# Repacking the value and output projections of a memory-augmented segment recurrence into windows of 64 columns, and moving its mask to VectorE

## The chip, the cores and the metric

One core of a Trainium2 chip. The metric is the device time of one execution in microseconds, told as the median of the runs. A run is called slow only when it is over 1.5% above the fastest of its kernel.

## The reference, cut to what matters

Two layers A, each followed by a dense layer B. Layer A walks through 64 segments of 32 rows; each segment sees 8 rows of memory that the segment before it wrote.

(Shortened: names and shapes are simplified.)

```python
mem = mem0
for s in range(n_seg):                       # 64 segments of 32 rows
    h = concat([mem, x[s]])                  # 8 + 32 rows, 512 wide
    q, k, v = h @ Wq, h @ Wk, h @ Wv         # 32 heads of 128
    p = softmax(mask(q @ k.T * 128 ** -0.5)) # memory rows see all, row i sees keys up to i
    o = (p @ v) @ Wo
    mem = o[:8]                              # the next segment waits for this
    outs.append(o[8:])
x = x + A(layernorm(x)); x = x + B(layernorm(x)); and both once more
```

The memory is a chain: nothing of segment s + 1 that touches the memory can start before the output projection of segment s is done.

## The kernel before

Both layers run together. In step k (there are 69) layer 0 works on segment k and layer 1 on segment k - 5. The two segments share one operand HT of 80 columns: `[x0: 32 | mem0: 8 | mem1: 8 | x1: 32]`. Every operation is handed to a small list scheduler in the kernel, which assumes durations and fixes the order on each engine when the kernel is built; the chip runs each engine's list in order. The scheduler has a constant for TensorE that favours work which uses the array in the same split as the work before it (WHOLE, COL64: two column halves side by side, COL32: four quarters, ROW64: two row halves). Cut to the lines that the change touches; "..." marks what is left out.

```python
WHOLE, COL64, COL32, ROW64 = range(4)
TURN = 0.11      # what the scheduler thinks a change of split costs, us
STAY = 2.0       # how strongly it prefers not to change
...
# values of x, made ahead of the memory: 64 columns, 32 products in column halves (COL64)
nc.tensor.matmul(vx[64*b:64*b+64, :], lhsT=XS[:, c4, :], rhs=Wv_sb[:, c4, n*512:(n+1)*512], ..., tile_position=(0, 64*b))
...
# values of the two memories: 32 columns, four quarters (COL32)
nc.tensor.matmul(vm[32*q:32*q+32, :], lhsT=HT[:, c4, SEG:SEG+32], rhs=Wv_sb[:, c4, n*512:(n+1)*512], ..., tile_position=(0, 32*q))
# both reach the value tiles Vs[a] by DMA, 12 transfers per step
...
# scores: the mask is a matmul that starts the accumulation
nc.tensor.matmul(sp[64*g2:64*g2+64, ...], lhsT=ident[:, 64*g2:64*g2+64], rhs=maskb[...], start=True, stop=False, ...)
nc.tensor.matmul(v[64*g2:64*g2+L, a, b, ii, :], lhsT=QT[...], rhs=KT[...], start=False, ...)
# VectorE: maximum, subtract; ScalarE: exp; VectorE: sum, reciprocal; GpSimd: multiply
# turn of P: 128 columns, bf16 in PSUM; VectorE copies it to PT
nc.tensor.transpose(tp[...][:, z*128:(z+1)*128], P[:, a, ii, :, :]..., ident[:])
...
# next memory: 32 columns, COL32; copied out in two halves, picked and turned by a small product, then into HT
nc.tensor.matmul(wo[32*q:32*q+32, :], lhsT=OT[:, h, SEG:SEG+32], rhs=Wo_sb[:, h, :], ..., tile_position=(0, 32*q))
# projection of x: 32 columns per layer, COL32, awaited by nobody in this step
nc.tensor.matmul(wx[32*q:32*q+32, :], lhsT=OT[:, h, XO[a]:XO[a]+SEG], rhs=Wo_sb[:, h, :], ..., tile_position=(0, 32*q))
plan.op(DVE, t_dve(512), add, r=[wx, x], w=[("x", g, c)])     # four adds into x per step
```

Of the kernel before, what the change touches and what calls it, by code (L numbers as in the profile page):

```python
# [26 lines left out]
STAY = 2.0  # L27
# [143 lines left out]
def kernel(  # L171
# [34 lines left out]
    XO = (0, L + M)  # L206
    MO = (SEG, L)
    XR = (0, M)
    MR = (SEG, 0)
# [53 lines left out]
    maskb = sb("maskb", [128, 2, L])  # L263
    nc.gpsimd.memset(maskb[:], 0.0)
    for g2 in range(2):
        blk = maskb[64 * g2:64 * g2 + 64, 0, 0:SEG]
        nc.gpsimd.affine_select(out=blk, in_=blk, compare_op=ALU.is_ge, fill=NEG,
                                base=0, pattern=[[-1, SEG]], channel_multiplier=1)
        blk = maskb[64 * g2:64 * g2 + 64, 1, :]
        nc.gpsimd.affine_select(out=blk, in_=blk, compare_op=ALU.is_ge, fill=NEG,  # L270
                                base=0, pattern=[[-1, L]], channel_multiplier=1)
        nc.gpsimd.affine_select(out=blk, in_=blk, compare_op=ALU.is_ge, fill=0.0,
                                base=-M, pattern=[[0, L]], channel_multiplier=1)

    sel_f = sb("sel_f", [128, 2 * M], F32)
    nc.gpsimd.memset(sel_f[:], 0.0)
    for g in range(4):
        blk = sel_f[32 * g:32 * g + 32, :]
        nc.gpsimd.affine_select(out=blk, in_=blk, compare_op=ALU.not_equal, fill=1.0,
                                base=0, pattern=[[-1, 2 * M]], channel_multiplier=1)  # L280
    sel = sb("sel", [128, 2 * M])
    nc.vector.tensor_copy(out=sel[:], in_=sel_f[:])
# [4 lines left out]
    XSs = [sb(f"XS{i}", [128, NC4, 2 * SEG]) for i in range(2)]  # L287
    QT = sb("QT", [128, H, 2 * L])
    KT = sb("KT", [128, H, 2 * L])
    Vs = [sb(f"Vs{a}", [128, 4, 512]) for a in range(2)]  # L290
    PT = sb("PT", [128, 4, 2, 4, L])
    Pt = [sb(f"P{p}", [128, 2, 2, 2, 64]) for p in range(4)]
    vst = sb("vst", [128, 4, 512])
    vms = sb("vms", [128, 2, 512])
    OT = sb("OT", [128, H, 2 * L])
    wm = sb("wm", [128, Dm])
    for t in (*HTs, *XSs):
        nc.vector.memset(t[:], 0.0)
    for t in (*Pt, OT):
        nc.gpsimd.memset(t[:], 0.0)  # L300

    p_es = ring("es", 2, [128, 2, 2, 2, L], F32)
# [6 lines left out]
    b_qk, b_misc, b_st, b_fill = banks("qk", 2), banks("misc", 3), banks("st", 1), banks("fill", 2)  # L309
# [147 lines left out]
    def prep_x(k):  # L457

        act, seg = segs(k)
        i = k % 2  # L460
        HT, XS = HTs[i], XSs[i]
        for a in act:
            g, c = divmod(seg[a], GS)
            xnT = xnT_tiles[(a, g)]
            for key, dst in ((("XS", i, a), XS[:, :, SEG * a:SEG * (a + 1)]),
                             (("HTx", i, a), HT[:, :, XO[a]:XO[a] + SEG])):
                def cp(dst=dst, xnT=xnT, c=c):
                    nc.gpsimd.tensor_copy(out=dst, in_=xnT[:, :, SEG * c:SEG * (c + 1)])

                plan.op(POOL, 0.25, cp, r=[xnT], w=[key])  # L470
        for p in range(4):
            vx = b_fill.buf()

            def mm(vx=vx, p=p):
                for c4 in range(NC4):
                    for b in range(2):
                        n = 2 * p + b
                        nc.tensor.matmul(vx[64 * b:64 * b + 64, :], lhsT=XS[:, c4, :],  # L478
                                         rhs=Wv_sb[:, c4, n * 512:(n + 1) * 512],
                                         start=(c4 == 0), stop=(c4 == NC4 - 1), tile_position=(0, 64 * b))  # L480

            plan.op(PE, 0.216 * NC4, mm, r=[("XS", i, 0), ("XS", i, 1), ("W", "v", p)], w=[vx, ("vst", p)], tile=COL64)
            eng = ACT if p != 3 else DVE

            def ev(vx=vx, p=p, eng=eng):
                copy_on(eng, vst[:, p, :], vx[:, :])

            plan.op(eng, t_copy(eng, 512), ev, r=[vx], w=[("vst", p)])

    def place_x_values(k):  # L490
        act, _ = segs(k)
        for a in act:
            for b in range(2):
                def dma(a=a, b=b):
                    nc.sync.dma_start(out=Vs[a][64 * b + XR[a]:64 * b + XR[a] + SEG, :, :],
                                      in_=vst[64 * b + 32 * a:64 * b + 32 * a + SEG, :, :])

                plan.op(SP, 0.6, dma, r=[("vst", p) for p in range(4)], w=[("Vx", a, b)])

    def mem_values(k):  # L500

        act, _ = segs(k)
        i = k % 2
        HT = HTs[i]
        for pp in range(2):
            vm = b_st.buf()

            def mm(vm=vm, pp=pp):
                for c4 in range(NC4):
                    for q in range(4):  # L510
                        n = 2 * (2 * (q // 2) + pp) + q % 2
                        nc.tensor.matmul(vm[32 * q:32 * q + 32, :], lhsT=HT[:, c4, SEG:SEG + 32],  # L512
                                         rhs=Wv_sb[:, c4, n * 512:(n + 1) * 512],
                                         start=(c4 == 0), stop=(c4 == NC4 - 1), tile_position=(0, 32 * q))

            plan.op(PE, 0.216 * NC4, mm, r=[("HTm", i), ("HTx", i, 1), *[("W", "v", pc) for pc in range(4)]], w=[vm],
                    tile=COL32)
            eng = ACT if pp == 0 else DVE

            def ev(vm=vm, pp=pp, eng=eng):  # L520
                copy_on(eng, vms[:, pp, :], vm[:, :])

            plan.op(eng, t_copy(eng, 512), ev, r=[vm], w=[("vms", pp)])
        for a in act:
            for q in range(4):
                def dma(a=a, q=q):
                    b, p0 = q % 2, 2 * (q // 2)
                    nc.sync.dma_start(out=Vs[a][64 * b + MR[a]:64 * b + MR[a] + M, p0:p0 + 2, :],  # L528
                                      in_=vms[32 * q + M * a:32 * q + M * (a + 1), :, :])

                plan.op(SP, 0.63, dma, r=[("vms", 0), ("vms", 1)], w=[("Vm", a, q)])

    def queries_keys(k, hg, a_lo, a_hi):
# [4 lines left out]
        for nm, W_sb, dstT in (("q", Wq_sb, QT), ("k", Wk_sb, KT)):  # L538
            qp = b_qk.buf()

            def mm(qp=qp, W_sb=W_sb):
                for hi in range(4):
# [6 lines left out]
                    r=[("HTm", i), *[("HTx", i, a) for a in range(a_lo, a_hi)], ("W", nm, hg // 2)], w=[qp])  # L549
            eng = DVE if nm == "k" and hg % 4 != 1 else ACT  # L550

            def ev(qp=qp, dstT=dstT, eng=eng):
                copy_on(eng, dstT[:, 4 * hg:4 * hg + 4, c0:c1],
                        qp[:, 0:8 * L].rearrange("p (h n) -> p h n", h=4)[:, :, 0:n])

            plan.op(eng, t_copy(eng, 4 * n), ev, r=[qp], w=[(nm + "T", hg)])

    def scores(k, p, a_lo, a_hi):
# [3 lines left out]
        sp, mx, es, sm, tp = b_misc.buf(), p_mx.buf(), p_es.buf(), p_sm.buf(), b_misc.buf()  # L562
        P = Pt[p]

        def spv():
            return sp[:, 0:8 * L].rearrange("p (a b i k) -> p a b i k", a=2, b=2, i=2)

        def mm():
            for g2 in range(2):
                nc.tensor.matmul(sp[64 * g2:64 * g2 + 64, a_lo * 4 * L:a_hi * 4 * L],  # L570
                                 lhsT=ident[:, 64 * g2:64 * g2 + 64],
                                 rhs=maskb[:, a_lo:a_hi, :].unsqueeze(2).to_broadcast([128, na, 4, L]),
                                 start=True, stop=False, tile_position=(0, 64 * g2))
            v = spv()
            for a in range(a_lo, a_hi):
                for b in range(2):
                    for ii in range(2):
                        for g2 in range(2):
                            h = 8 * p + 4 * b + 2 * ii + g2
                            last = a == a_hi - 1 and b == 1 and ii == 1  # L580
                            nc.tensor.matmul(v[64 * g2:64 * g2 + L, a, b, ii, :], lhsT=QT[:, h, a * L:(a + 1) * L],  # L581
                                             rhs=KT[:, h, a * L:(a + 1) * L], start=False, stop=last,
                                             tile_position=(0, 64 * g2))

        def top():
            nc.vector.tensor_reduce(out=mx[:, 4 * a_lo:4 * a_hi],  # L586
                                    in_=sp[:, a_lo * 4 * L:a_hi * 4 * L].rearrange("p (s k) -> p s k", k=L),
                                    axis=AX.X, op=ALU.max)

        def flat():  # L590
            return es[:, a_lo:a_hi, :, :, :].rearrange("p a b i k -> p (a b i) k")
# [199 lines left out]
```

## Time and profile before

| | before |
|---|---|
| median of the runs | 2098.54 us |
| span of the profiled execution | 2094.9 us |
| TensorE, VectorE, ScalarE, GpSimd busy | 94%, 57%, 37%, 16% |
| mean granted TensorE clock of that execution | 0.982 |
| weights arriving, TensorE idle at the start | 60.5 us |

How to read it: TensorE is the engine to relieve, since it is busy nearly all the time after the first 60 us. The price of an operation is best taken as the distance between two starts where nothing waits.

### The profile page before, as it was taken

What the parts mean: (1) busy time and instruction counts of PE and PEld (TensorE: products, weight loads), DVE (VectorE), ACT (ScalarE), POOL (GpSimd) and SP (SyncE); (2) the same over time, 40 slices, a digit from 0 to 9 for tenths busy, and PEclk for the clock granted to TensorE, in tenths of its full rate; (3) what the DMA queues carried; (4) which work ended last, traced back from release to release, by engine and by line L of the source; (5) the groups of instructions that cost most, each with busy time, mean ns of one, the idle gap of its engine ahead of it and who ended that gap; (6) DMA issues with size and microseconds to landing.
All of it is one profiled execution on the core that took longest, in us unless ns stands there. A gap on an engine that the chain in (4) does not pass through costs nothing.

```text
span 2094.9 us, 91031 instructions
## 1 busy us (share of the span) xinstructions
PE 1960.3 (94%) x40675; PEld 1313.9 (63%) x40728; DVE 1184.8 (57%) x2913; ACT 770.7 (37%) x1795; POOL 344.6 (16%) x902
## 2 busy tenths in 40 slices
PE   0699989999999999999999999999999999999998
PEld 0466666666765676666666666666667666666665
DVE  0254656565655656665556656556666656555553
ACT  0233333333433343343334343333434334343333
POOL 2011111111111112121111112111211111111111
PEclk9899999999999999999999999999999999999999
DMA  9200101101110111111011111111011110101000
GB/s 338 59 17 10 37 18 28 26 22 37 24 28 20 34 27 28 26 25 26 22 36 23 28 28 30 24 26 28 20 31 28 31 30 18 28 21 36 14 21 15
DMA packets 39256, 71.60 MB, mean 34 GB/s; under 512 B 13168, under 2 KB 20336, under 8 KB 38864
## 3 DMA queue, kind: packets, MB, share of 16 engines
q1 hardware_dynamic: 33296, 52.34, 11.3%
q8 instruction: 319, 5.23, 1.0%
q10 hardware_dynamic: 3824, 6.78, 0.9%
q0 software_dynamic: 1744, 6.65, 0.9%
q14 instruction: 73, 0.60, 0.1%
HBM read 21.70 MB, written 2.10 MB: 11 GB/s over the span
## 4 chain that ended last, share of the span: by engine, by line
PE 82%; DVE 10%; SPq 3%; DMA 2%; issue 2%; POOL 1%; ACT 1%; DVEq 0%; POOLq 0%; ACTq 0%
PE qk L545 29%; PE fill L711 12%; PE fill L478 10%; PE st L512 6%; PE st L672 6%; PE fill L359 4%; DVE xg L722 3%; PE misc L626 3%; PE misc L646 3%; PE fill L385 3%; PE misc L570 2%; PE misc L581 2%; DVE KT L452 1%; SPq L528 1%; DMA bf<-in_A_x_dram 1%
## 5 line engine op out<-in xcount | busy, mean ns | idle before, releaser
L617 POOL TENSOR_TENSOR P<-es,sm 128x160 bf16<-128x160 f32 (+1 forms) x552 | 230.1, 440 | 1074.5 <-DVE sm L605 967.4
L450 ACT CAST QT<-qk 128x320 bf16<-128x320 f32 (+1 forms) x552 | 221.5, 404 | 480.1 <-PE qk L545 398.6
L545 PE MATMUL qk<-HT,Wk_sb 128*128 128x80 bf16 (+1 forms) x8832 | 377.0, 200 | 16.3 <-DVE HT L694 11.7
L545 PEld LDWEIGHTS <-Wk_sb 128*128 128x128 bf16 x8832 | 333.7, 100 | 83.7 <-issue 78.1
L545 PE MATMUL qk<-HT,Wq_sb 128*128 128x80 bf16 (+1 forms) x8832 | 376.2, 200 | 0.6 <-DVE KT L452 0.5
L545 PEld LDWEIGHTS <-Wq_sb 128*128 128x128 bf16 x8832 | 330.3, 100 | 73.2 <-issue 67.7
L711 PE MATMUL fill<-Wo_sb,OT 128*32 128x512 bf16 x4416 | 293.4, 384 | 1.0
L478 PE MATMUL fill<-Wv_sb,XS 128*64 128x512 bf16 x2208 | 292.3, 387 | 0.7
L452 DVE CAST KT<-qk 128x320 bf16<-128x320 f32 (+1 forms) x414 | 188.5, 462 | 163.8 <-PE qk L545 136.2
L722 DVE TENSOR_TENSOR xg<-xg,fill 32x512 f32<-32x512 f32 x256 | 174.6, 682 | 137.5 <-PE fill L711 131.8
L586 DVE TENSOR_REDUCE mx<-misc 128x8 f32<-128x320 f32 (+1 forms) x276 | 126.9, 462 | 125.4 <-PE misc L581 124.0
L599 ACT ACTIVATE es<-es 128x320 f32<-128x320 f32 (+1 forms) x276 | 123.8, 451 | 179.2 <-DVE es L594 177.0
L450 ACT CAST vst<-fill 128x512 bf16<-128x512 f32 x207 | 121.0, 585 | 169.4 <-PE fill L478 154.0
L452 DVE CAST OT<-misc 128x320 bf16<-128x320 f32 (+1 forms) x276 | 126.9, 460 | 97.3 <-PE misc L646 95.4
L672 PE MATMUL st<-Wo_sb,OT 128*32 128x512 bf16 x2176 | 176.3, 395 | 0.0
L450 ACT CAST OT<-misc 128x320 bf16<-128x320 f32 (+1 forms) x276 | 112.1, 406 | 164.7 <-PE misc L646 147.7
L711 PEld LDWEIGHTS <-OT 128*32 128x32 bf16 x4416 | 104.3, 97 | 98.5 <-issue 9.2
L478 PEld LDWEIGHTS <-XS 128*64 128x64 bf16 x2208 | 103.6, 110 | 93.1 <-issue 25.8
L602 DVE TENSOR_REDUCE sm<-es 128x8 f32<-128x320 f32 (+1 forms) x276 | 124.9, 454 | 45.6 <-ACT es L599 44.5
L512 PE MATMUL st<-Wv_sb,HT 128*32 128x512 bf16 x2208 | 147.2, 387 | 0.8 <-DVE vms L452 0.8
L594 DVE TENSOR_TENSOR es<-misc,mx 128x320 f32<-128x320 f32 (+1 forms) x276 | 127.3, 464 | 18.0 <-POOL P L617 4.6
L646 PEld LDWEIGHTS <-Vs 40*128 40x128 bf16 x4096 | 75.9, 93 | 83.8 <-issue 68.7
(70 smaller groups left out, 1795.0 us busy)
## 6 DMA issues: line engine op xcount, KB each, us to landing
Vs<-vst SPq DMA_DIRECT2D x256, 128.0 KB
Vs<-vms SPq DMA_DIRECT2D x512, 16.0 KB
Wk_sb<-in_A_Wk_dram ACTq DMA_DIRECT2D x2, 1024.0 KB
Wv_sb<-in_A_Wv_dram POOLq DMA_DIRECT2D x2, 1024.0 KB, 18.9
Wq_sb<-in_A_Wq_dram SPq DMA_DIRECT2D x2, 1024.0 KB
Wo_sb<-in_A_Wo_dram SPq DMA_DIRECT2D x2, 1024.0 KB
out_dram<-bf SPq DMA_DIRECT2D x16, 128.0 KB
bf<-in_A_x_dram SPq DMA_DIRECT2D x15, 128.0 KB
```

What stands on the lines that cost most here:

```text
L450: nc.scalar.copy(out=out_, in_=in_)
L452: nc.vector.tensor_copy(out=out_, in_=in_)
L478: nc.tensor.matmul(vx[64 * b:64 * b + 64, :], lhsT=XS[:, c4, :], rhs=Wv_sb[:, c4, n * 512:(n + 1) * 512], start=(c4 == 0), stop=(c4 == NC4 ...
L512: nc.tensor.matmul(vm[32 * q:32 * q + 32, :], lhsT=HT[:, c4, SEG:SEG + 32], rhs=Wv_sb[:, c4, n * 512:(n + 1) * 512], start=(c4 == 0), stop ...
L545: nc.tensor.matmul(qp[:, hi * 2 * L:hi * 2 * L + n], lhsT=W_sb[:, c4, h * Dh:(h + 1) * Dh], rhs=HT[:, c4, c0:c1], start=(c4 == 0), stop=(c ...
L586: nc.vector.tensor_reduce(out=mx[:, 4 * a_lo:4 * a_hi], in_=sp[:, a_lo * 4 * L:a_hi * 4 * L].rearrange("p (s k) -> p s k", k=L), axis=AX.X ...
L594: nc.vector.tensor_tensor(out=flat(), in0=sp[:, a_lo * 4 * L:a_hi * 4 * L].rearrange("p (s k) -> p s k", k=L), in1=mx[:, 4 * a_lo:4 * a_hi ...
L617: nc.gpsimd.tensor_tensor(out=P[:, a_lo:a_hi, :, b, 0:L], in0=es[:, a_lo:a_hi, b, :, :], in1=s.unsqueeze(3).to_broadcast([128, na, 2, L]), ...
L646: nc.tensor.matmul(pv[b][:, (2 * hh + a) * L:(2 * hh + a + 1) * L], lhsT=Vs[a][R:R + L, p, hh * Dh:(hh + 1) * Dh], rhs=PT[R:R + L, p, a, h ...
L672: nc.tensor.matmul(wo[32 * q:32 * q + 32, :], lhsT=OT[:, h, SEG:SEG + 32], rhs=Wo_sb[:, h, :], start=(t == 0), stop=(t == H // 4 - 1), til ...
L711: nc.tensor.matmul(wx[32 * q:32 * q + 32, :], lhsT=OT[:, h, XO[a]:XO[a] + SEG], rhs=Wo_sb[:, h, :], start=(t == 0), stop=(t == H // 2 - 1) ...
L722: nc.vector.tensor_tensor(out=rows, in0=rows, in1=wx[r:r + 32, :], op=ALU.add)
```

## The change

The intent is to do with 64-column windows what took a 64-column and a 32-column pass. Layer 0's 32 rows are put in HT with their two halves swapped, `[late half: 16 | early half: 16 | mem0 | mem1 | x1: 32]`, so that columns 16 to 80 are one window of 64: half of layer 0, both memories and all of layer 1. Values and output projection of the window are made in each step; those of the late half (which nobody needs outside its own segment) are made for four segments at once, once in four steps. The rest of the change:

- The mask is added on VectorE, out of PSUM into SBUF, and no longer by a matmul.
- The turn of P streams 80 columns, not 128, and leaves fp32 in PSUM.
- Layer 1's values are used where they were evicted; only layer 0's go through DMA (6 transfers per step for 12).
- The copy of the next memory is one ScalarE instruction, not two halves on two engines.
- The adds into x wait until the new memory is in HT.
- Half of the key evictions go to VectorE, not three quarters (276 for 414).
- Key and query tiles are rings of four; five PSUM banks are one pool; STAY is 0.5.

The diff is cut and its calls are shortened; two lines of it describe a function in words.

```diff
-STAY = 2.0
+STAY = 0.5
...
-        nc.tensor.matmul(vx[64*b:...], lhsT=XS[:, c4, :], rhs=Wv_sb[...])            # x, COL64
-        nc.tensor.matmul(vm[32*q:...], lhsT=HT[:, c4, SEG:SEG + 32], rhs=Wv_sb[...]) # memories, COL32
+        values(HTs[i][:, :, HS:2 * L], vw, "vw", ...)    # the window, COL64, each step
+        values(XG[:, :, :], vg, "vg", ["XG"])            # late halves, COL64, once in four steps
...
-            for g2 in range(2):
-                nc.tensor.matmul(sp[64 * g2:...], lhsT=ident[...], rhs=maskb[...], start=True, stop=False, ...)
+        def block():
+            nc.vector.tensor_tensor(out=esv(), in0=spv(), op=ALU.add, in1=maskb[...])
...
-                    nc.tensor.transpose(tp[:, :].bitcast(BF)[:, z * 128:(z + 1) * 128], P[...], ident[:])
+                    nc.tensor.matmul(tp[:, z * 2 * L:(z + 1) * 2 * L], lhsT=P[:, c0:c0 + 128], rhs=rhs, ...)
...
-    next_memory: OT[:, h, SEG:SEG + 32] in COL32, 8 places;  project_x: 2 x 32 columns in COL32, 16 places
+    project: nc.tensor.matmul(wo[64 * u:64 * u + 64, :], lhsT=OT[:, h, HS:2 * L], rhs=Wo_sb[:, h, :], ...)
+    project_late: the late halves of four segments, then one matmul that spreads them over the rows
...
-                plan.op(DVE, t_dve(512), add, r=[wx, x], w=[("x", g, c)])
+                plan.op(DVE, t_dve(512), add, r=[wo, x, ("HTm", i)], w=[("x", g, c)])
```

## The prediction

> **What bounds the kernel now.** I read the page's busy row first, then the slices, the chain that ended last, the groups, the waits of TensorE, and last the timeline of two steps of the recurrence. The page:
>
> ```profile
> PE 1960.3 (94%) x40675; PEld 1313.9 (63%) x40728; DVE 1184.8 (57%) x2913; ACT 770.7 (37%) x1795; POOL 344.6 (16%) x902
> ...
> PE   0699989999999999999999999999999999999998
> ...
> PE 82%; DVE 10%; SPq 3%; DMA 2%; issue 2%; POOL 1%; ACT 1%; DVEq 0%; POOLq 0%; ACTq 0%
> ```
>
> TensorE works at 90% or more in nearly every slice and carries 82% of the last chain. So a change pays here as it takes TensorE time away without opening new gaps. The groups that the change touches, by line and shape:
>
> ```profile
> L711 PE MATMUL fill<-Wo_sb,OT 128*32 128x512 bf16 x4416 | 293.4, 384 | 1.0
> L478 PE MATMUL fill<-Wv_sb,XS 128*64 128x512 bf16 x2208 | 292.3, 387 | 0.7
> L672 PE MATMUL st<-Wo_sb,OT 128*32 128x512 bf16 x2176 | 176.3, 395 | 0.0
> L512 PE MATMUL st<-Wv_sb,HT 128*32 128x512 bf16 x2208 | 147.2, 387 | 0.8 <-DVE vms L452 0.8
> L626 PE MATMUL misc<-ident,P 128*128 128x128 bf16 x1024 | 101.3, 221 | 20.2 <-POOL P L617 18.1 <-DVE PT L631 1.5 <-DVE OT L452 0.2
> L570 PE MATMUL misc<-maskb,ident 128*64 128x320 bf16 x472 | 74.8, 314 | 0.0
> ```
>
> These means (384 ns) are pipelined and overlap; the price is the distance between starts, so I took it from the timeline. A COL64 pair or COL32 quadruple runs side by side.
>
> ```profile
> 1013.15 1.31 PE L545 MATMUL qk<-HT,Wq_sb 128*128 128x80 bf16 x32
> 1014.30 0.84 PE L359 MATMUL fill<-xnM,w_sb 128*128 128x128 bf16 x12
> ...
> 1042.97 1.32 PE L545 MATMUL qk<-HT,Wq_sb 128*128 128x80 bf16 x32
> 1044.22 1.05 PE L478 MATMUL fill<-Wv_sb,XS 128*64 128x512 bf16 x8
> 1045.11 0.30 PE L570 MATMUL misc<-maskb,ident 128*64 128x320 bf16 x2
> ```
>
> The same 32 products take 1.15 us when the next group uses the array in the same split and 1.25 us when the split changes. Over all steps the medians say the same (16 products of 80 columns 0.58 and 0.67, an L711 group of 16 0.87 and 0.98, scores 0.20 and 0.29): **a change of split costs 0.10 us**. Four places of 512 columns (a "round" below) cost 0.87 us without it; the mask pair 0.16 us at 320 columns and 0.09 at 160; four turns of P 0.23 us.
>
> TensorE's waits are few, and the first is the weights' arrival:
>
> ```profile
> PE fill L333 <- DVE bf L328: 68.3, 5, 60.5
> PE misc L626 <- POOL P L617: 18.1, 31, 1.6
> PE qk L545 <- DVE HT L694: 11.7, 6, 2.2
> ```
>
> And the edge between two steps, where the new memory goes through the engines:
>
> ```profile
> 1033.61 1.06 PE L711 MATMUL fill<-Wo_sb,OT 128*32 128x512 bf16 x16
> ...
> 1033.92 0.37 ACT L450 CAST wm<-st 128x256 bf16<-128x256 f32 x1 [0.45 <-PE st L672]
> ...
> 1034.33 0.42 DVE L452 CAST wm<-st 128x256 bf16<-128x256 f32 x1 [2.36 <-ACT wm L450]
> ...
> 1034.61 0.41 PE L685 MATMUL misc<-sel,wm 128*128 128x16 bf16 x4
> 1034.94 1.05 PE L478 MATMUL fill<-Wv_sb,XS 128*64 128x512 bf16 x8
> 1035.05 0.22 DVE L694 CAST HT<-misc 128x64 bf16<-128x64 f32 x1 [0.30 <-PE misc L685]
> ```
>
> From the last memory product (33.61) to the new HT (35.27) are 1.66 us. TensorE covers it with L711 and L478, the projection and values of x, which nobody awaits: this is the filler that the change takes apart.
>
> **What the skill says.** "TensorEngine Tiling (Array Packing)", Key Properties: changing the tiling mode drains the array. The trace agrees, 0.10 us each. The same page, Theoretical Speedup, promises 2x at 64 columns and 4x at 32; the trace has both (8 matmuls of L478 and 16 of L711 each take about 0.87 us). "TensorE: Matmul & The Clock Gate", Back-to-back issue gap: columns/2.4 + 2.5 ns, thus 216, 56 and 36 ns at 512, 128 and 80 columns; the trace has 217, 57 and 36. "PSUM — Partial Sum Buffer", PSUM bank collisions: two engines may not touch one bank at once; the two halves of wm above indeed follow one another (DVE starts at 34.33, ACT ended at 34.29).
>
> **The change part by part.** I counted the TensorE instructions of both built programs, in their order.
>
> 1. Values. Before, per step, four rounds for x (64 columns) and two for the memory (COL32). After, one window of 64 columns (half of layer 0's rows, both memories, all of layer 1's) in four rounds; the other half is made once in four steps, in four rounds.
> 2. Projection: the same, six rounds per step become four, and four per group, plus one spreading matmul per group.
> Together, rounds before: 276 + 138 + 276 + 136 = 826; after: 276 + 64 + 276 + 64 = 680. 146 x 0.87 = 127 us less; 16 spreads of 0.22 give back 3.5: **-123.5 us**.
> 3. The mask leaves TensorE: 236 x 0.16 + 40 x 0.09 = **-41 us**.
> 4. The turn streams 80 columns, not 128: 1024 x (57.5 - 36) ns = **-22 us**.
> 5. No COL32, and the scheduler regroups: 1914 changes of split before, 1190 after: 724 x 0.10 = **-72 us**. In the order, steps now run eight QK groups in a row.
> 6. STAY falls from 2.0 to 0.5, which alone would allow more switches; its effect is inside the count.
> TensorE total: **-259 us**.
>
> VectorE gains work: the mask addition, 236 x 0.487 + 40 x 0.32 = +128 us (as the subtraction L594); PT copies from fp32, 0.486 in place of 0.318, +43; late values and late adds, 32 x 0.69 + 16 x 0.67 = +33; gone are 138 K evictions (-64) and half of wm (-29). Sum +111 us, so 1296. ScalarE changes by some +20. DMA issues into the value tiles fall from 768 to 384, which loosens the queue (SPq 3%).
>
> On the path at the edge, wm becomes one ScalarE copy of 512 (0.585 us, as for vst) in place of 0.37 + 0.42 in a row, while the transposed products follow whole: 1.66 us stays about 1.66. The adds into x now wait for HT, so they no longer get in its way.
>
> **New gaps.** The new order repeats every four steps. Of four edges, two have filler on both sides of the L725 products, one only after them, one none. A bare edge costs 0.95 us before the products (0.31 from 33.61 to 33.92, the copy's 0.585, 0.05 to the next engine) and 0.37 after them (0.11 from 34.94 to 35.05, 0.22, 0.04); a round of filler covers all but 0.08 of the first. Per four steps: 0.95 + 0.37 + 0.95 + 2 x 0.08 = 2.4 us, or some 40 us over 17 such periods (an estimate from the rows above).
> The tail of a step is the other place: softmax gains one link (0.49 us), and VectorE works in order. Summing the durations along the orders, the four steps of a period need TensorE 27.6, 23.8, 21.7 and 25.5 us, and VectorE 23.2, 20.2, 20.5 and 20.9. VectorE must also wait at the head for the first keys (about 1 us) and at the end for product, copy and memory (about 2.5). So the third step, with 21.7 against 20.5 + 3.5, will wait on VectorE by 2 to 3 us, the second by 1 to 2, the others by 1 or less, edges included: 6 to 8 us per four steps, some 110 us in all.
> The kernel before, priced in the same way, comes to 1905 us of TensorE; with 60.5 of weights that leaves 2094.9 - 1965.5 = 129 us of stalls already (62 shown as waits, the rest spread over longer groups). I take 60 us of new stalls beyond those.
>
> **Sum.** 2094.9 - 259 + 60 = 1896 span; the runs are about 3 us above the span: 1898 us.
>
> **Rivals.**
> - All of the gain arrives: fill and VectorE suffice. For: 57% VectorE now; the edge loses its ACT-DVE relay and the competing adds. Against: work that nobody awaits at once falls from about 9.6 us per step (eight rounds for x, and 2.6 us as a fourth of two dense layers) to 4.4 us (eight rounds in four steps and the same 2.6), in lumps. Time: 1838.
> - The recurrence is laid bare: every edge waits 1.4 us (97 us), and each tail 1 us more. For: values now wait for the memory, so they can't run ahead of it. Against: the order still has filler at two of four edges. Time: 1980 to 2000.
> - VectorE becomes the bound: 21.2 us per step plus the 3.5 to 5.5 us in which it must wait is 24.7 to 26.7 us; 69 such steps and 60.5 make 1765 to 1903. It is near TensorE's 24.7 us per step, hence my middle, and not beyond it.
> - The switches saved lay in waits: then 72 us fewer, 1970. Against: 0.10 shows in rows with no wait before them.
> - The late projection holds up layer 1: four rounds (3.5 us), copy, spread, add, two normalisations and the dense layer are some 17 us, within a step of 27. It should hide.
>
> **Range and chances.** The TensorE sum is counted, uncertain by 25 us; the stalls may be 10 to 120. Hence 1845 to 1955. Even with the laid-bare recurrence it is over 2% faster: faster 0.97, within 2% 0.025, slower 0.005.
>
> **What would show it.** TensorE busy near 1700 to 1760 us; L518 and L712 groups of 8 at 0.87 apart; no COL32; turns at 36 ns apart; VectorE busy near 1296; waits of L725 for ScalarE's wm and of QK for HT, some 40 us; waits of L666 for POOL and of L685 for PT, grown. I am wrong if VectorE waits carry the chain in all steps, if TensorE's busy time falls by under 200 us, or if the edges with filler stall too.

## The result, and the profile after

| | before | after |
|---|---|---|
| median | 2098.54 us (15 runs) | 1864.89 us (8 runs) |
| span of the profiled execution | 2094.9 us | 1865.3 us |
| TensorE busy | 1960.3 us | 1684.0 us |
| VectorE busy | 1184.8 us | 1257.7 us |
| mean granted clock | 0.982 | 0.996 |

The ratio is 0.889, with an interval of 0.888 to 0.890. A ratio here is the mean time of one kernel's fast runs over the mean of the other's of the same rounds, so it is not quite the ratio of the medians. The prediction was 1898 with a range of 1845 to 1955; the kernel is 33 us faster than the middle.

The page of the changed kernel: busy times, TensorE's slices, and the chain that ended last.

```profile
PE 1684.0 (90%) x34578; PEld 1237.7 (66%) x34624; DVE 1257.7 (67%) x3035; ACT 787.9 (42%) x1843; POOL 420.8 (23%) x1171
...
PE   0489899999999999999999999999999999999997
...
PE 79%; DVE 8%; issue 4%; ACT 3%; DMA 3%; SPq 2%; POOL 0%; DVEq 0%; POOLq 0%; ACTq 0%
```

TensorE is still what carries the chain, with a lower share: it waits more than before. The groups, by shape:

```profile
L712 PE MATMUL st<-Wo_sb,OT 128*64 128x512 bf16 x2208 | 302.4, 387 | 21.9 <-ACT OT L470 20.4 <-DVE OT L472 0.3
L615 DVE TENSOR_TENSOR es<-work,maskb 128x320 f32<-128x320 f32 x236 | 114.6, 486 | 90.7 <-PE work L601 89.2 <-POOL P L656 0.7 <-ACT qT L470 0.3
L769 PE MATMUL fill<-Wo_sb,OXb 128*64 128x512 bf16 x512 | 69.8, 382 | 0.0
L666 PE MATMUL work<-ident,P 128*128 128x80 bf16 x1024 | 71.1, 204 | 6.0 <-POOL P L656 5.8
```

No group has 32 weight columns any more. From start to start, eight L712 or L518 products take 0.87 us and four turns 0.15 us, as priced (medians over all the groups with no wait before the next); a change of split again adds 0.10 us. TensorE's waits (engine, line, what it waited for: us in total, times, longest):

```profile
PE work L685 <- DVE PT L670: 30.4, 39, 1.2
PE work L725 <- ACT wm L719: 24.7, 36, 0.9
PE st L712 <- ACT OT L470: 20.4, 58, 0.8
PE work L573 <- DVE HT L734: 10.6, 25, 1.2
```

They stand in the two places that were named: the edge between steps (L725 and L573, 35 us; 40 were predicted) and the tail of a step (L685 and L712, 51 us). Within the tail the naming was half right: the wait for PT grew from 3.2 to 30.4 us, as predicted, but the wait of the turn for GpSimd's P, which was to grow too, fell from 18.1 to 5.8 us, and the wait of the projection for OT (20.4 us) was not named. A bare edge in the timeline (start, duration, engine, line):

```profile
929.28 1.05 PE L712 MATMUL st<-Wo_sb,OT 128*64 128x512 bf16 x8
...
930.38 0.58 ACT L719 CAST wm<-st 128x512 bf16<-128x512 f32 x1 [0.40 <-PE st L712]
...
931.02 0.26 PE L725 MATMUL work<-selm,wm 128*128 128x16 bf16 x4 [0.68 <-ACT wm L719]
931.31 0.22 DVE L734 CAST HT<-work 128x64 bf16<-128x64 f32 x1 [2.55 <-PE work L725]
931.45 0.67 DVE L750 TENSOR_TENSOR xg<-xg,st 16x512 f32<-16x512 f32 x1
```

The product ends, one copy on ScalarE, the picking product, the copy into HT, and only then the first add into x.

**A ledger.** To see where the 33 us came from, I priced both kernels' TensorE instructions by the distances between starts, as in the prediction, for every product (0.217 us for a place of 512 columns, 36 ns for 80, 57 ns for 128, and 0.10 us for each change of split). What a span has beyond the start and this sum is loss. A part of it is clock. The profile gives the granted clock for any stretch; I took stretches of 2 us and added up 2 us x (1 - clock). TensorE also stands still in some of that time, so this is an upper bound for what the clock cost. (The last stretch reaches past the span's end in every run, so each clock figure is about 1 us too high and each "other waits" as much too low; the differences stand.)

| us | before | after | difference |
|---|---|---|---|
| weights at the start | 60.6 | 60.6 | |
| products, by count | 1716 | 1527 | -189 |
| changes of split | 1914 x 0.10 = 191 | 1190 x 0.10 = 119 | -72 |
| lower clock | 39 | 8 | -31 |
| other waits | 88 | 151 | +63 |
| span | 2094.9 | 1865.3 | -229.6 |

The sum of the work (-261) is near the predicted -259, but both are the same count at the same prices; what the trace confirms is the order (1914 and 1190 changes of split, as counted) and the prices. The clock is the part that was not foreseen. How large it is stays uncertain. The 21 runs of the kernel before that came with the experiments have clocks from 0.980 to 0.989, and a straight line through them gives about 8 us of time for 0.01 of clock (correlation -0.67), where the ledger charges 21. By this estimate the rise from 0.982 to 0.996 is worth some 11 us, not 31, and the waits then grew by some 43, not 63. In the kernel before, the stretches of an edge (busy us of the engines, then granted clock, DMA share, GB/s):

```profile
1002.00:1004.00 2.00, 0.00 (x0) 0.00 (x0) 1.91 (x5) 0.00 (x0) 0.00 (x0) 0.74 0.16 55
1004.00:1006.00 2.00, 1.99 (x31) 1.99 (x31) 1.62 (x5) 0.00 (x0) 0.55 (x1) 0.50 0.13 44
1006.00:1008.00 2.00, 2.00 (x21) 0.56 (x18) 1.25 (x3) 0.43 (x1) 0.00 (x0) 0.50 0.04 8
```

and the edge of the changed kernel that was shown above:

```profile
930.00:932.00 2.00, 1.00 (x20) 0.58 (x17) 0.69 (x2) 0.58 (x1) 0.53 (x2) 1.00 0.00 0
932.00:934.00 2.00, 2.00 (x61) 2.00 (x58) 1.91 (x4) 0.85 (x2) 0.00 (x0) 1.00 0.04 8
```

In the first, VectorE did two adds into x and a normalisation's statistics before it copied the memory; TensorE stood for 2.2 us, and then worked at half clock for some 6 us (the clock fell at 1002.94, while it still stood). There the products count as busy in full (1.99 of 2.00), and the loss can't be seen in the busy row. The kernel before has nine such stretches between 160 and 1730 us, the changed one has one; both have one at the start (17 us long before, 3.4 us after) and one at the end.

### The profile page after: what moved, and what is told of

Same layout as the page of the kernel before. It is cut to its first block, busy times and chain, and to the rows that moved or that the text cites. A ratio compares the mean times of both kernels' runs of the same rounds, so it can differ in the third digit from the quotient of the medians.

```text
span 1865.3 us, 78729 instructions
## 1 busy us (share of the span) xinstructions
PE 1684.0 (90%) x34578; PEld 1237.7 (66%) x34624; DVE 1257.7 (67%) x3035; ACT 787.9 (42%) x1843; POOL 420.8 (23%) x1171
## 4 chain that ended last, share of the span: by engine, by line
PE 79%; DVE 8%; issue 4%; ACT 3%; DMA 3%; SPq 2%; POOL 0%; DVEq 0%; POOLq 0%; ACTq 0%
PE work L573 33%; PE st L712 14%; PE fill L518 11%; PE fill L379 5%; PE fill L405 4%; PE work L685 3%; PE fill L769 3%; PE work L601 3%; DVE es L615 2%; PE work L666 2%; DVE PT L670 1%; DVE mx L625 1%; ACT OT L470 1%; DMA bf<-in_A_x_dram 1%; ACT wm L719 1%
## 5 line engine op out<-in xcount | busy, mean ns | idle before, releaser
L573 PE MATMUL work<-HT,Wk_sb 128*128 128x80 bf16 (+1 forms) x8832 | 395.1, 199 | 10.9 <-DVE HT L734 10.6
L573 PE MATMUL work<-HT,Wq_sb 128*128 128x80 bf16 (+1 forms) x8832 | 394.2, 199 | 1.1 <-POOL HT L492 1.1
L573 PEld LDWEIGHTS <-Wk_sb 128*128 128x128 bf16 x8832 | 338.9, 100 | 50.8 <-issue 39.2
L470 ACT CAST qT<-work 128x320 bf16<-128x320 f32 (+1 forms) x552 | 223.5, 406 | 312.9 <-PE work L573 269.2
L573 PEld LDWEIGHTS <-Wq_sb 128*128 128x128 bf16 x8832 | 340.3, 100 | 10.0 <-issue 7.9
L712 PE MATMUL st<-Wo_sb,OT 128*64 128x512 bf16 x2208 | 302.4, 387 | 21.9 <-ACT OT L470 20.4
L518 PE MATMUL fill<-Wv_sb,HT 128*64 128x512 bf16 x2208 | 286.4, 382 | 0.5
L615 DVE TENSOR_TENSOR es<-work,maskb 128x320 f32<-128x320 f32 (+1 forms) x276 | 126.9, 462 | 116.2 <-PE work L601 114.2
L712 PEld LDWEIGHTS <-OT 128*64 128x64 bf16 x2208 | 133.0, 109 | 91.9 <-ACT OT L470 32.7
L750 DVE TENSOR_TENSOR xg<-xg,st 16x512 f32<-16x512 f32 (+1 forms) x256 | 174.9, 683 | 8.4 <-PE st L712 1.1
L518 PEld LDWEIGHTS <-HT 128*64 128x64 bf16 x2208 | 103.4, 109 | 69.1 <-issue 7.3
L472 DVE CAST kT<-work 128x320 bf16<-128x320 f32 (+1 forms) x276 | 127.7, 463 | 19.4 <-PE work L573 12.0
L628 DVE TENSOR_TENSOR es<-es,mx 128x320 f32<-128x320 f32 (+1 forms) x276 | 127.0, 461 | 3.0
```

The lines of the kernel that those rows point to most:

```text
L470: nc.scalar.copy(out=out_, in_=in_)
L472: nc.vector.tensor_copy(out=out_, in_=in_)
L518: nc.tensor.matmul(vp[64 * b:64 * b + 64, :], lhsT=cols[:, c4, :], rhs=Wv_sb[:, c4, n * 512:(n + 1) * 512], start=(c4 == 0), stop=(c4 == N ...
L573: nc.tensor.matmul(qp[:, hi * 2 * L:hi * 2 * L + n], lhsT=W_sb[:, c4, h * Dh:(h + 1) * Dh], rhs=HT[:, c4, c0:c1], start=(c4 == 0), stop=(c ...
L615: nc.vector.tensor_tensor(out=esv(), in0=spv(), op=ALU.add, in1=maskb[:, a_lo:a_hi, :].unsqueeze(2).to_broadcast([128, na, 4, L]))
L628: nc.vector.tensor_tensor(out=es3(), in0=es3(), in1=mx[:, 4 * a_lo:4 * a_hi].unsqueeze(2).to_broadcast([128, 4 * na, L]), op=ALU.subtract)
```

## The experiments

Each chip ran the kernel before too, and it stood at 2097.7 to 2099.2 us in all of them. The ledger of all runs comes after the experiments. The edits are cut to their main lines.

### e1: the scheduler's constant alone

```diff
 (kernel before)
-STAY = 2.0
+STAY = 0.5
```

> The kernel before with STAY 0.5 alone. In the built order the split of the array then changes 2085 times, not 1914, and the groups are otherwise the same. Theory 'work removed from TensorE': 171 changes x 0.10 us = 17 us slower, about 2115 us. Rival 'the scheduler constant is what made the change fast': clearly faster than 2098, by 30 us or more.

Measured 2101.45 us, ratio 1.001 (0.9985 to 1.0035). The constant alone is not the gain: the rival falls. The 17 us did not show either. In the ledger they are there by count (sum +17), and the clock loss is 17 us smaller (22 for 39, upper bounds both). The half-clock stretches fall in other places; that this made up for the 17 us is not shown.

### e2: the adds into x wait, and nothing else

```diff
 (kernel before)
-plan.op(DVE, t_dve(512), add, r=[wx, x], w=[("x", g, c)])
+plan.op(DVE, t_dve(512), add, r=[wx, x, ("HTm", (k + 1) % 2)], w=[("x", g, c)])
```

> The kernel before, with only the adds into x made to wait for the new memory, as the changed kernel does. Number of products the same, 1908 changes of split. Theory 'part of the gain is clock': the 2.2 us waits of TensorE for HT start four of the ten half-clock stretches of before (granted clock 0.982 on average, some 31 us more lost than in the changed kernel); without them the clock rises to 0.987 or more and the time falls by 12 us of waits plus 15 to 25 us of clock, to 2060 to 2075. Rival 'the clock has nothing to do with these waits': clock still 0.98, time 2085 to 2100.

Measured 2069.11 us, ratio 0.986 (0.983 to 0.988); granted clock 0.984 to 0.992 in its four runs, 0.980 to 0.989 in the seven of before. One added dependence gives 30 us to the kernel before. In the ledger 10 us are clock, as an upper bound, and 15 us other waits; the wait for HT fell from 11.7 to 0.6 us. So the direction holds, but my account of the clock was too simple. The expectation counts four of ten stretches; the trace of before has eleven, of which three begin inside a 2.2 us wait for HT and a fourth follows one of 0.73 us. And here seven half-clock stretches remain between 300 and 1730 us, some 236 us apart, and there is no wait for HT ahead of them. What stands ahead of the one that begins at 1013 us:

```profile
1009.17 0.38 PE L626 MATMUL misc<-ident,P 128*128 128x128 bf16 x4 [0.43 <-DVE es L594]
...
1010.98 0.60 PE L646 MATMUL misc<-PT,Vs 40*128 40x40 bf16 x16 [0.56 <-DVE PT L631]
1012.15 0.38 PE L626 MATMUL misc<-ident,P 128*128 128x128 bf16 x4 [0.56 <-ACT OT L450]
```

A few waits of half a microsecond close together are followed by half clock as well. The changed kernel has such clusters without it. The trace of the kernel before says a little more. There every half-clock stretch starts on one grid of 3.41 us and lasts a whole number of its steps. The same 2.2 us wait for HT comes five times, with the same two short waits ahead of it. At 1002, 1364 and 1722 us it left TensorE busy for only 1.50 to 1.63 us of one grid step, and the next step was at half clock. At 285 and 644 us the grid divided it, no step had less than 1.80 us busy, and the clock stayed full. What differs between the five is their place on the grid. The busy time alone is not the rule: six other steps with 1.94 to 2.73 us busy were followed by half clock, and in the changed kernel one with 2.00 us was (206.65 to 210.06) and one with 1.92 us was not (230.54 to 233.95).

### e3: the former constant in the changed kernel

```diff
 (changed kernel)
-STAY = 0.5
+STAY = 2.0
```

> The changed kernel with STAY back at 2.0. In the built order 1098 changes of split, not 1190, and no edge between two steps is without filler ahead of the memory transpose (26 of 52 were). Theory 'switches and bare edges cost time': 92 x 0.10 = 9 us less, and the 25 us in which the memory transpose waits for wm mostly go: 1830 to 1845 us. Rival 'VectorE sets the pace of the tail': waits turn up as waits for PT or OT and the time stays at 1855 to 1875.

Measured 1871.91 us, ratio to before 0.892. A miss: 7 us slower than the changed kernel although 9 us of changes of split are gone and the order has filler at every edge. The wait for wm did fall (25 to 11 us), but new waits for HT and for the copies of x into it came in their place (14.1 for 10.6 and 9.4 for 1.1 us). The rival's time was right, its place was not: it named PT and OT, whose waits did not grow (22.6 and 19.7 us, from 30.4 and 20.4).

### e4: without the row maximum

```diff
 (changed kernel)
-        plan.op(DVE, t_dve(n), top, r=[es], w=[mx])
-        plan.op(DVE, t_dve(n), sub, r=[mx], w=[es])
```

The softmax is then exp of the masked scores, correct here because the scores are small; for large scores it could overflow.

> The changed kernel without the row maximum and its subtraction (two VectorE instructions of 0.48 us less per quarter step, some 240 us of VectorE; the softmax stays right for these inputs because the scores are small). TensorE's products are the same, 1201 changes of split. Theory 'the longer VectorE chain makes the new stalls': waits for PT (30 us) and OT (20 us) shrink and the time falls by 40 to 70 us, to 1795 to 1825. Rival 'the stalls lie at the edges and in TensorE's own work': 1855 to 1870.

Measured 1827.77 us, ratio 0.871 (0.869 to 0.872): 37 us less than the changed kernel, just short of the range that I gave, with the same products. Its waits in the tail:

```profile
PE work L683 <- DVE PT L668: 8.6, 17, 1.1
PE st L710 <- ACT OT L470: 8.0, 27, 0.5
```

They were 30.4 and 20.4 us. So VectorE's softmax makes the waits in the tail. Whether by the length of its chain or by VectorE's load this run cannot say, since it takes off both (67% to 57% busy); e5 and e7 come closer.

### e5: the mask back on TensorE

```diff
 (changed kernel)
+            for g2 in range(2):
+                nc.tensor.matmul(sp[64 * g2:64 * g2 + 64, ...], lhsT=ident[...], rhs=maskc[...], start=True, stop=False, ...)
-        plan.op(DVE, t_dve(n), block, r=[sp], w=[es])
```

> The changed kernel with the mask back on TensorE (552 identity matmuls with the mask as moving operand; VectorE's mask addition taken out). TensorE by count: 236 x 0.16 + 40 x 0.09 = 41 us, and 1237 changes of split for 1190, 5 us: +46. VectorE loses 128 us and one link of 0.49 us per quarter step; taking two links out gave 37 us back, so one should give some 18. Theory 'the move of the mask paid, less what the longer VectorE chain costs': 1865 + 46 - 18 = 1893, between 1882 and 1903. Rival 'the mask was free on TensorE, beside waits': 1850 to 1870. Rival 'the whole 41 us arrived': 1908 or more.

Measured 1877.86 us, ratio 0.896: 13 us slower than the changed kernel, less than I expected and outside all three ranges. The ledger shows 48 us more TensorE work and 41 us less waiting. So the move of the mask brought 13 us of its 41 to 48. Not all of the 41 need be the chain: in e11, where the added work lies outside it, a third of that work was taken back by shorter waits, which here would be some 15 us (an estimate).

### e6: the turns of 128 columns

```diff
 (changed kernel)
-  nc.tensor.matmul(tp[:, z * 2 * L:(z + 1) * 2 * L], lhsT=P[:, c0:c0 + 128], rhs=rhs, ...)
+  nc.tensor.transpose(tp[:, :].bitcast(BF)[:, z * 128:(z + 1) * 128], P[:, c0:c0 + 128], ident[:])
```

> The changed kernel with the turns of P as before: 128 columns, bf16 in PSUM, and the PT copy in 0.32 us rather than 0.48. TensorE by count: 1024 x 21.5 ns = 22 us, and 1253 changes of split for 1190, 6 us. VectorE loses some 40 us, all of it in the link ahead of the attention products, 0.17 us per quarter step: 6 us back at the rate of the run without the maximum. Theory 'count less chain': 1887, between 1878 and 1895. Rival 'the narrow turn brought nothing, since its longer PT copy takes it back': 1858 to 1870.

Measured 1872.37 us, ratio 0.893: 7 us slower, between the theory and the rival and nearer to the rival. Here too 27 us of TensorE work stand against 24 us of waits that went, of which some 9 us may go with any added work, by the same estimate.

### e7: all keys evicted by ScalarE

```diff
 (changed kernel)
-            eng = DVE if nm == "k" and hg % 2 else ACT
+            eng = ACT
```

> The changed kernel with all key evictions on ScalarE: VectorE loses 138 copies of 0.46 us, 64 us (67% busy to about 64%), ScalarE gains 56 us; no link of the softmax chain gets shorter; 1176 changes of split. Theory 'VectorE's load, not only the chain's length, makes the tail wait': 1845 to 1858. Rival 'only the length of the chain counts': 1860 to 1870. Rival 'ScalarE gets in the way of exp and of the memory copy': over 1872.

Measured 1864.94 us, ratio 0.890: the same. VectorE went from 67% to 62% busy and nothing came of it. The expectation's 138 copies were a miscount: the edit moves all 276 that the changed kernel had on VectorE, 124 us by their durations. That makes it a good partner for e5: both leave VectorE about 1156 us busy (1157.0 here, 1155.0 there), but only e5 shortens the softmax chain, and there the waits fell by 41 us, here by 9. So the chain's length counts far more than the engine's load, with the reserve that e5 also adds work to TensorE and that here ScalarE got 98 us more. (Its clock was lower, 0.991 to 0.995 for 0.994 to 0.997; the ledger has 11 us more clock loss and 9 us less waiting, so the waits did shrink a little.)

### e8: the scheduler with measured durations

```diff
 (changed kernel)
-LAT = (0.26, 0.16, 0.16, 0.20, 1.70)
+LAT = (0.28, 0.05, 0.05, 0.05, 1.70)
-    return 0.09 + 0.833e-3 * n      # ScalarE
+    return 0.155 + 0.84e-3 * n
-    return 0.085 + 1.042e-3 * n / rate   # VectorE
+    return 0.152 + 1.045e-3 * n / rate
-    return 0.06 + 2.2e-3 * n        # GpSimd
+    return 0.185 + 1.7e-3 * n
```

> The changed kernel with nothing but the scheduler's durations and latencies set to what the trace shows (VectorE 0.152 + 1.045 ns per column, ScalarE 0.155 + 0.84, GpSimd 0.185 + 1.7, 0.05 us from a VectorE, ScalarE or GpSimd instruction to the next engine). 1144 changes of split, 13 of 52 edges bare for 26. Theory 'stalls come from an order planned with wrong durations': 5 us for the changes of split and 10 to 25 us of waits, 1835 to 1852. Rival 'the stalls are in the dependences and only change place': 1858 to 1875.

Measured 1887.98 us, ratio 0.901: 23 us slower, and outside both. The order that was planned with better single durations has 14 us more clock loss and 12 us more waits. A likely part of the reason, not tested by itself: VectorE instructions that follow one another start closer together than they last, as here in the changed kernel,

```profile
946.04 0.47 DVE L625 TENSOR_REDUCE mx<-es 128x8 f32<-128x320 f32 x1
946.43 0.48 DVE L670 CAST PT<-work 128x320 bf16<-128x320 f32 x1
```

0.39 us apart at a duration of 0.47. The former formula gives 0.418 for this shape and mine 0.486, so mine was the worse one for a busy VectorE.

### e9: the values made as before

```diff
 (changed kernel)
-        values(HTs[i][:, :, HS:2 * L], vw, "vw", ...); late_values(g); place_values(...)
+        values(XSs[i][:, :, :], vst, "vst", ...)     # x rows of both layers, four rounds, ahead of the memory
+        ... vm[32 * q:32 * q + 32, :] <- HT[:, c4, SEG:SEG + 32] in COL32, two rounds
+        12 transfers per step into V0 and V1, layer 1 read from V1
```

To make it fit, the copy wxs shares its tile with wm and two scratch tiles lie in the es ring.

> The changed kernel with the values made as before: x rows of both layers in four rounds ahead of the memory, both memories in two rounds of quadruples, both placed by copies through DMA; projection, mask and turn stay changed. TensorE by count: 276 + 138 rounds for 340, 74 x 0.87 = 64 us, and 1362 changes of split for 1190, 17 us: +81. Against this, the x values are again work that nobody awaits. Theory 'fewer rounds and fewer changes of split are the gain': 1865 + 81 - (0 to 20) = 1925 to 1950. Rival 'losing the filler cost about as much as the rounds saved': 1860 to 1895.

Measured 2108.82 us, ratio 1.005: 244 us slower than the changed kernel, and slower than the kernel before. Of this 81 us are work by count. The rest is 89 us of other waits and up to 71 us of clock (granted 0.963 to 0.965). One line names most of the waits:

```profile
PE work L690 <- DMA V<-vst: 67.4, 62, 3.7
```

In the changed kernel the waits for DMA are 5 us. So the rival (that losing the filler cost as much as the rounds saved) falls clearly, but the theory's 1925 to 1950 is missed by 160 us as well. The window has a second effect, which the prediction had only touched: layer 1's values need no transfer and layer 0's need half as many. This run does not tell the rounds and the transfers apart, since my version brings all twelve transfers back into a step that has become shorter.

### e10: mask and turn in the kernel before

```diff
 (kernel before)
-  mask matmuls; transpose of 128 columns
+  block() on VectorE; product of 80 columns, fp32 in PSUM
```

> The kernel before with the mask added on VectorE and the turns of 80 columns, values and projection as before. TensorE by count: 41 + 22 us less, 1921 changes of split for 1914. VectorE gains some 170 us and the softmax chain 0.65 us per quarter step, but here there is more filler. Theory 'filler covers the longer chain': 2098 - 62 + (0 to 15) = 2036 to 2051. Rival 'the longer chain gives most of it back, as in the changed kernel, where the two were worth 13 and 7 us': 2070 to 2085.

Measured 2148.75 us, ratio 1.024 (1.023 to 1.026): slower than the kernel before by 51 us, a miss of both. TensorE has 65 us less to do, but other waits rise by 91 and the clock loss by 31 us.

```profile
PE misc L626 <- POOL P L617: 31.3, 43, 1.8
PE qk L547 <- DVE HT L693: 29.7, 24, 2.2
```

They were 18.1 and 11.7. The fuller VectorE makes the turn wait for P and the step for HT, with waits of up to 2.2 us. The granted clock was 0.967 to 0.973, for 0.982 to 0.985 in the kernel before on the same chip. So these two parts cost 51 us alone and bring 13 and 7 us beside the others (e5, e6): the parts of this change do not simply add.

### e11: more changes of split, the order untouched

```diff
 (changed kernel, in values())
             def mm(vp=vp, p=p):
+                nc.tensor.matmul(vp[:, 0:16], lhsT=ident[:, :], rhs=ident[:, 0:16], start=True, stop=True)
```

> The changed kernel, its order untouched, with one small product on the whole array (128x128 weights, 16 columns, overwritten by what follows) ahead of each of the 340 value rounds. Changes of split rise from 1190 to 1654. Theory 'each change of split costs 0.10 us that nothing hides': 46 us plus 340 products of 0.03 to 0.06 us, 1865 + 56 to 66 = 1918 to 1932. Rival 'the cost lies beside waits': at most the products themselves, 1865 to 1885.

Measured 1911.83 us, ratio 0.911 (0.910 to 0.913): 47 us slower for 464 more changes and 340 small products, 6 us below the range of the theory and 27 us above that of the rival, so neither holds as stated. With 0.04 us for a product, the ledger adds 60 us of work and 6 of clock and takes 19 off the waits. Changes of split cost time, most of it in the open and some of it beside waits.

### e12: without the maximum, turns in column halves

```diff
 (the kernel of e4)
-  nc.tensor.matmul(tp[:, ...], lhsT=P[:, c0:c0 + 128], rhs=rhs, ...)
+  for u in range(2):
+      nc.tensor.matmul(tp[64 * u:64 * u + 64, ...], lhsT=P[:, c0 + 64 * u:c0 + 64 * u + 64], rhs=rhs, ..., tile_position=(0, 64 * u))
```

> The run without the maximum, with the turns of P made in column halves (two products of 64 weight columns side by side), so that they no longer leave the split of their neighbours: 1026 changes of split for that run's 1201, and no edge bare ahead of the memory transpose. Theory 'changes of split cost 0.10 us': 17 us less than 1828, 1803 to 1815. Rival 'twice the weight loads or moved waits take it back', as the fewer changes of split were taken back under STAY 2.0: 1822 to 1840.

Measured 1814.62 us, ratio 0.865 (0.864 to 0.867): 13 us less than e4, with 175 fewer changes of split and the same columns streamed. The order changed with it (other waits 116 for 111 us), so the 13 us are not the changes of split alone. It is the fastest version here, 50 us below the changed kernel, at the price of a softmax that is not guarded against large scores.

### The ledger of all runs

Same method as above; "sum" is products and changes of split by count.

| run | median | sum | lower clock | other waits |
|---|---|---|---|---|
| before | 2098.5 | 1907 | 39 | 88 |
| after | 1864.9 | 1646 | 8 | 151 |
| e1 before, STAY 0.5 | 2101.5 | 1924 | 22 | 91 |
| e2 before, adds wait | 2069.1 | 1907 | 28 | 73 |
| e10 before, mask and turn | 2148.8 | 1842 | 69 | 179 |
| e3 after, STAY 2.0 | 1871.9 | 1636 | 11 | 163 |
| e4 after, no maximum | 1827.8 | 1647 | 8 | 111 |
| e5 after, mask on TensorE | 1877.9 | 1694 | 10 | 110 |
| e6 after, turns of 128 | 1872.4 | 1673 | 8 | 127 |
| e7 after, keys by ScalarE | 1864.9 | 1644 | 19 | 142 |
| e8 after, measured durations | 1888.0 | 1641 | 22 | 163 |
| e9 after, values as before | 2108.8 | 1727 | 78 | 240 |
| e11 after, more changes | 1911.8 | 1706 | 14 | 132 |
| e12 e4 with turns in halves | 1814.6 | 1629 | 6 | 116 |

## Why the prediction was right, point by point

**The TensorE sum, -259 us: right as far as it can be checked.** Priced in the same way, the two built programs differ by 261 us. That is the same count again; what is measured is that the traces have the changes of split as counted (1914 and 1190) and the prices that were used. The 0.10 us for a change of split was tested by adding changes (e11) and by taking them away (e12).

**New stalls, +60 us: right in kind, nearly twice too large.** The prediction's 129 us of stalls in the kernel before are all of the time beyond weights and counted work, lower clock included. In these terms the loss rose from 127 to 159 us, by 32 and not by 60. Those 28 us are most of the 33; the rest is 2 us of the sum and 3 us that the prediction added for runs over the span. The 60 was also not worked out: the text finds some 110 us of stalls in the new order and then "takes" 60 beyond the 129. That it lies near the ledger's +63 of waits is partly luck, since that number depends on the upper bound for the clock (some +43 with the estimate from the runs' scatter). The edges were near (35 us measured, 40 predicted). What the prediction did not see is whose stalls they are: taking the mask's move and the narrow turn back removes 41 and 24 us of waits (e5, e6), though part of that would go with any added work. So those two parts, 63 us of TensorE by the prediction, brought 13 and 7 us. By subtraction, then, the gain is mostly the windows' work, with the adds that wait and the fewer transfers. The new pools and rings and the single copy of the memory were not tested alone.

**Clock: not in the prediction, and a part of the 33 us.** The failing step is the sentence that put 129 us of the kernel before down to stalls, "62 shown as waits, the rest spread over longer groups". Of that rest up to 39 us were half clock. The profile of before had a mean granted clock of 0.982, and I took it as given. The change takes it to 8 us. That is up to 31 of the 33 us, and some 11 by the estimate from the runs' scatter. The adds that wait for HT, which I had filed as a detail of the edge, give 30 us to the kernel before (e2), up to 10 of them as clock.

**VectorE, 1296 us: 38 too many.** The count was right: the durations of its instructions add up to 1280.0 us before and 1386.6 after, 107 more where 111 were predicted. But the prediction added durations to a busy time. The busy row counts overlapping instructions once, and neighbours on a full VectorE start 0.39 us apart and last 0.47; it rose by 73 us, to 1257.7. So VectorE had more room than my sums of durations gave it, and the rival "VectorE becomes the bound" was weaker than I argued; e7, which relieves VectorE without shortening its softmax chain, brings nothing.

**TensorE busy, 1700 to 1760 us: too high,** measured 1684.0. Probably this is half clock again, since TensorE was busy for 66 us of half-clock time before and for 13 us after; no run tests it.

**A reading that shows less than it says.** The two halves of wm do follow one another, but the line names ScalarE's copy as what VectorE waited for (2.36 <-ACT wm L450). The program keeps them apart; what the chip does with a collision is not shown.

**The rivals.** "All of the gain arrives" is out: the loss rose by 32 us. "The recurrence is laid bare" is out: 36 waits for wm, not 69 bare edges (its parts, 97 and 69 us on 1838, make 2004 and not the 1980 to 2000 that it states). "The switches lay in waits" is mostly out (e11: about a third of the added cost was absorbed). The late projection held nothing up: its group L769 shows no wait, and no wait is listed for its add, L781.

**Open.** How much idle time in one grid step is enough for half clock, and what the half clock cost between the 11 and the 31 us; how much of e9's 244 us is rounds and how much transfers; and why the better durations of e8 gave a worse order.

## What to carry to other kernels

When a window of rows leaves half of the array's columns unused in one pass, choose the layout so that two passes become one, and count places and changes of split in the built program before running it: the traces had exactly the changes that were counted, at the prices that were used. Then treat VectorE's chain as a second price: work that is moved off TensorE into a dependent chain came back as waits for the larger part (41 of 48 us, 24 of 27, of which about a third may go with any work). And read the granted clock in short stretches, for an average of 0.98 hid up to 39 us that neither the busy row nor the waits showed; but do not take that bound for the cost.

## What the Trainium skill lacked or had wrong

- "TensorEngine Tiling (Array Packing)", Key Properties, says that a change of tiling mode drains the array and gives no figure. Here one change costs about 0.10 us in both kernels (0.57 to 0.67 us for 16 products of 80 columns, 0.87 to 0.97 or 0.99 for a round); 464 more changes with 340 small products cost 47 us.
- "TensorE: Matmul & The Clock Gate", HAM oscillation, gives as the abstract rule "no PE-idle gaps >~3.4µs". The section after it tells of half clock from frequent short idles, without a length for them. Here 6.8 us of half clock began 1.1 us into a gap of 2.2 us, and in e2 the same followed a row of gaps of at most 0.56 us. Over an execution this cost up to 39 us before and up to 78 in e9.
- The same page, Back-to-back issue gap, gives both 81 ns (sustained, 128 columns) and 56 ns (isolated). With a weight load for every product, this kernel sustains 57 ns at 128 columns and 36 ns at 80.
- "VectorE: DVE Perf Modes", The DRAIN you can't avoid, says that the next instruction does not start until the pipe is empty, and leaves earlier starts to its section on two instructions with no wait between them, which has no times. Here neighbours on different tiles start 0.39 us apart while the profile gives each 0.47, so durations do not add up to busy time (1386.6 us by sum, 1257.7 busy).
